# Attention with a sliding window and two MLPs: DVE's copy of the transposed probabilities and its reciprocals in front of the weight split, one more copy on ACT

## The chip, the cores and the metric

One core of one Trainium2 chip. The metric is the device time of one execution in microseconds, as the median of three runs.

## What is computed

```python
def _attn_ref(q, k, v, n_sink, window):          # q, k, v: 2 x 8 x 768 x 64; n_sink 4, window 128
    scores = np.matmul(q, k.transpose(0, 1, 3, 2)) / np.sqrt(D)
    keep = is_sink | in_window                   # the first 4 keys, and the 128 up to the query's own
    scores = np.where(keep, scores, -1e9)
    a = np.exp(scores - np.max(scores, axis=-1, keepdims=True))
    a = a / (np.sum(a, axis=-1, keepdims=True) + 1e-09)
    return np.matmul(a, v)

def reference(...):
    x = attn_out as 1536 tokens x 512
    h = x @ w_in;  g = elu(h);   x = g @ w_out      # 512 -> 2048 -> 512, first MLP
    h = x @ w_in2; g = max(h,0) + alpha*min(h,0)    # second MLP
    return g @ w_out2
```

The weights arrive as 64-bit floats.

## The kernel before

Queries are cut into seven blocks of 110 (the last has 108). Attention works on **units**: one or two query blocks of one pair of heads. There are 32 of them. Block 6 is a unit by itself, so units 9 and 11, for example, have one block, while units 8 and 10 have two. Each block gives two tiles, one for each head of the pair.

`fast_path` runs a loop of 34 **steps**, in an order written out by hand: each engine takes its instructions in the order in which the program issues them. In step s three units are at work:

- Unit s: PE forms the scores (L521, tiles `qk`, four PSUM buffers). DVE scales, masks and takes the maximum of each tile (L529). ACT takes the exponential and its sum (L534). Then `normalised` has DVE add 1e-9 and take the reciprocal (L544, L547, tile `st`), and POOL multiplies each tile of probabilities `s` by it (L551), two multiplications for a unit of one block and four for a unit of two.
- Unit s-1: `transposed` has PE transpose its probabilities into PSUM (L565, `t`), one tile a block. Each is copied to SBUF (`pt`, L649): the first copy of a unit on DVE, the second on ACT up to step `DS[HP]`, that is step 9, and on DVE after that.
- Unit s-2: `values` multiplies `pt` by the values (L586, `x`). ACT rounds the product to the high part (`xh`, L594), DVE takes the rest (`xl`, L596).

Beside these a step takes one piece of the first MLP from a list (`fill`): from step 5 to 12 one tile of `h` (L293, twelve matmuls; `g1`), whose ELU runs on ACT (L325, L326) and DVE (L327, tile `u`), and from step 13 on a tile of `o` (`g2`). Where there is no such piece PE is kept busy with matmuls that nothing reads. ACT rounds `u` to `gh` (L339) and POOL forms the rest `gl` (L340) at the start of the next step.

The weights of the first quarter of the first MLP are split in the same loop, eight **half slices** of 128x512, in the steps `DS = [1, 3, 5, 7, 9, 10, 11, 12]`. `decode_w` turns 64-bit floats into two 32-bit parts, high and low. It is a generator, and its pieces are issued at these places: at the end of step s-1 two operations on ACT (L267, L268), in step s four operations on DVE (L270, L273, L276, L279; tiles `wx`, `wq`), called **the split** here, and at the start of step s+1 the rounding on ACT (`wh`, L283) and the rest on DVE (`wl`, L285). On DVE the `wl` of step s stands in front of the first L529 of step s+1. The `o` of step 13 needs the half slice that is split in step 12.

On DVE a step of the list `DS` thus reads: L529 (two or four times), L596, the split, L649, L544, L547, L327, then L285 of the start of the next step. The attention and its list end near 165 us. After that the two MLPs run over token groups of 512.

Of the kernel before, what the change touches and what calls it, by code (L numbers as in the profile page):

```python
# [34 lines left out]
HP = H // 2  # L35
# [21 lines left out]
DS = [1, 3, 5, 7, 9, 10, 11, 12]  # L57
# [56 lines left out]
def attention_mlp2(  # L114
# [13 lines left out]
    nc = tc.nc  # L128
# [64 lines left out]
    def load_w(m, fc, io, raw=None):  # L193
        if raw is None:
            raw = rawp.tile([P, DM, 2], I32, tag="raw", name=f"wr{m}_{fc}_{io}")
        nc.sync.dma_start(
            out=raw, in_=weights[m][fc, io].bitcast(I32).rearrange("p (n t) -> p n t", t=2)
        )
        wraw[m, fc, io] = raw
# [18 lines left out]
    for i, most in enumerate((SINK, 0, WIN, 0)):  # L218
# [7 lines left out]
        out=flag_i, in0=int1[:, 2:3].bitcast(U32), scalar=0.5, in1=flag_m, op0=ALU.is_ge, op1=ALU.mult  # L226
# [6 lines left out]
        out=lims, in0=intf[:, :, 0], scalar=0.0, in1=intf[:, :, 1], op0=ALU.is_lt, op1=ALU.add  # L233
    )
    nc.vector.scalar_tensor_tensor(
        out=lims, in0=lims, scalar=4294967296.0, in1=intf[:, :, 0], op0=ALU.mult, op1=ALU.add
# [10 lines left out]
    def keep_busy(pool, tag, n):  # L247

        t = pool.tile([P, 512], F32, tag=tag, name=f"busy{next(ids)}")
        for _ in range(n):  # L250
            nc.tensor.matmul(t[:, :P], ident, ident, start=True, stop=True)  # L251
# [121 lines left out]
    def done(steps):  # L373
        for _ in steps:
            pass
# [116 lines left out]
    def fast_path():  # L492
# [13 lines left out]
        def scores(i):  # L506
            g, blks = units[i]
            z = sgs[g][1]
            nk, nq = KTOT[z], QTOT[z]
            sb = at.tile([P, UB, 2, WMAX], F32, tag="s", name=f"s{i}", bufs=SB)  # L510
            st = at.tile([P, 4, UB, 2], F32, tag="st", name=f"st{i}", bufs=SB)
            pts = {}
            for blk in blks:
                n, (k0, w) = NQ[blk], SPAN[blk]
                for e in range(2):


                    pts[blk, e] = pt = ps_qk.tile([P, 512], F32, tag="qk", name=f"qk{i}_{blk}_{e}")
                    a = keys[g][e * D : e * D + D]
                    q0 = (nk if e == 0 else 2 * nk - nq) + Q0[blk] - Q0[SPLIT[z][0]]  # L520
                    nc.tensor.matmul(  # L521
                        pt[:n, :w], a[:, q0 : q0 + n], a[:, k0 : k0 + w], start=True, stop=True
                    )
            soft[i] = sb, st
            for j, blk in enumerate(blks):
                n, w = NQ[blk], KW[blk]
                mask = masks[mask_of[blk]]
                for e in range(2):
                    nc.vector.tensor_tensor_reduce(  # L529
                        out=sb[:n, j, e, :w], in0=pts[blk, e][:n, :w], in1=mask[:n, :w],  # L530
                        scale=-SCALE, scalar=3.0e38, op0=ALU.add, op1=ALU.min,
                        accum_out=st[:n, 0, j, e : e + 1],
                    )
                    nc.scalar.activation(  # L534
                        sb[:n, j, e, :w], sb[:n, j, e, :w], AF.Exp, bias=st[:n, 0, j, e : e + 1],
                        scale=-1.0, accum_out=st[:n, 1, j, e : e + 1],
                    )
                yield

        def normalised(i):  # L540
            _, blks = units[i]
            n, c = NQ[blks[0]], len(blks)
            sb, st = soft[i]
            nc.vector.tensor_scalar(  # L544
                out=st[:n, 2, :c], in0=st[:n, 1, :c], scalar1=1.0e-9, scalar2=None, op0=ALU.add
            )
            nc.vector.reciprocal(st[:n, 3, :c], st[:n, 2, :c])  # L547
            for j, blk in enumerate(blks):
                w = KW[blk]
                for e in range(2):  # L550
                    nc.gpsimd.tensor_scalar(  # L551
                        out=sb[:n, j, e, :w], in0=sb[:n, j, e, :w], scalar1=st[:n, 3, j, e : e + 1],
                        scalar2=1.0, op0=ALU.mult, op1=ALU.mult,
                    )

        def transposed(i):
            _, blks = units[i]
            sb, _ = soft.pop(i)
            for j, blk in enumerate(blks):
                n, c, r = NQ[blk], NCH[blk], CR[blk]  # L560
                tp = ps.tile([P, 512], F32, tag="ps", name=f"t{i}_{blk}")
                for e in range(2):
                    for k in range(c):
                        o = (e * c + k) * n
                        nc.tensor.transpose(  # L565
                            tp[:r, o : o + n], sb[:n, j, e, k * r : k * r + r], ident[:n, :n]
                        )
                pt = at.tile([P, 4 * QB], F32, tag="pt", name=f"pt{i}_{blk}", bufs=PB)
                trans[i, blk] = pt
                yield pt[:r, : 2 * c * n], tp[:r, : 2 * c * n]  # L570

        def values(i):
            g, blks = units[i]
            b, z, hp = sgs[g]
            vr = vals[g]
            px = ps.tile([P, 512], F32, tag="ps", name=f"x{i}")
            o = 0
            for blk in blks:
                n, c, r = NQ[blk], NCH[blk], CR[blk]
                v0 = sum(NCH[SPLIT[z][0] : blk]) * 2 * D  # L580
                pt = trans.pop((i, blk))
                for e in range(2):
                    for k in range(c):
                        vs = v0 + (k * 2 + e) * D
                        p0 = (e * c + k) * n
                        nc.tensor.matmul(  # L586
                            px[e * D : e * D + D, o : o + n], vr[:r, vs : vs + D], pt[:r, p0 : p0 + n],
                            start=(k == 0), stop=(k == c - 1),
                        )
                o += n  # L590
            c0 = b * S + Q0[blks[0]]
            xh, xl = (x[:, hp, c0 : c0 + o] for x in xs)

            nc.scalar.copy(xh, px[:, :o])  # L594
            yield
            nc.vector.tensor_tensor(out=xl, in0=px[:, :o], in1=xh, op=ALU.subtract)  # L596
# [27 lines left out]
        decodes = {}  # L624
        gates = []
        for s in range(nu + 2):
            late = s - 1 in decodes
            if late:
                next(decodes[s - 1])
            for a in gates:  # L630
                done(a)
            gates = []
            if late:
                done(decodes.pop(s - 1))
            sc = scores(s) if s < nu else iter(())
            next(sc, None)
            vs = values(s - 2) if s >= 2 else iter(())
            next(vs, None)
            done(sc)
            done(vs)  # L640
            if s in decodes:
                next(decodes[s])
            take = 1 if fill and fill[0][0] <= s else 0
            after = fill.pop(0)[1]() if take else None
            if not take and s < nu:
                keep_busy(ps, "ps", BUSYN)
            if 1 <= s <= nu:
                for j, (out, in_) in enumerate(transposed(s - 1)):
                    (nc.scalar.copy if j and s <= DS[HP] else nc.vector.tensor_copy)(out, in_)  # L649
            if s < nu:  # L650
                normalised(s)
            if not take and s < nu:
                keep_busy(ps, "ps", BUSYN)
            if after:
                after = after()
                next(after)
                gates.append(after)
            if len([f for f in fill if f[0] <= s]) >= FILL_MAX:
                after = fill.pop(0)[1]()()
                next(after)  # L660
                gates.append(after)
            for blk, at_ in MS.items():
                if s == at_:
                    make_mask(blk)
            if s + 1 in DS:
                decodes[s + 1] = decode_w(at2, wa, *ws[DS.index(s + 1)])
                next(decodes[s + 1])
            if s in DS and WPRE <= DS.index(s) and DS.index(s) + 3 < len(ws):
                load_w(*ws[DS.index(s) + 3])
            if s < nu:  # L670
                g = units[s][0]
                if s == last_of[g] and HP <= g and g + LB < len(sgs):
                    load_kq(g + LB, at)
            if s >= 2:
                g = units[s - 2][0]
                if s - 2 == last_of[g] and HP <= g and g + LB < len(sgs):
                    load_v(g + LB, at)
# [153 lines left out]
```

## Time and profile before

| | us |
|---|---|
| median of 3 runs | 660.78 |
| lowest and highest | 659.86, 787.24 |
| the profiled execution | 662.34 |
| its span in the trace | 660.5 |
| PE busy in the span | 633.7 (96%) |
| DVE busy | 435.9 (66%) |
| ACT busy | 315.7 (48%) |
| POOL busy | 204.4 (31%) |

PE's share is an average over the whole span. The steps of the list `DS` lie between 10.03 and 76.49 us, a tenth of it. The granted TensorE clock over the span is 0.986 of full speed.

### The profile page before, as it was taken

What the parts mean: (1) busy time and instruction counts of PE and PEld (TensorE: products, weight loads), DVE (VectorE), ACT (ScalarE), POOL (GpSimd) and SP (SyncE); (2) the same over time, 40 slices, a digit from 0 to 9 for tenths busy, and PEclk for the clock granted to TensorE, in tenths of its full rate; (3) what the DMA queues carried; (4) which work ended last, traced back from release to release, by engine and by line L of the source; (5) the groups of instructions that cost most, each with busy time, mean ns of one, the idle gap of its engine ahead of it and who ended that gap; (6) DMA issues with size and microseconds to landing.
All of it is one profiled execution on the core that took longest, in us unless ns stands there. A gap on an engine that the chain in (4) does not pass through costs nothing.

```text
span 660.5 us, 9670 instructions
## 1 busy us (share of the span) xinstructions
PE 633.7 (96%) x3444; PEld 526.6 (80%) x3444; DVE 435.9 (66%) x927; ACT 315.7 (48%) x719; POOL 204.4 (31%) x253
## 2 busy tenths in 40 slices
PE   8986899999989899999999999999999999999996
PEld 7775688887977677888888888888888888888885
DVE  5877767655399997768465876694669673343332
ACT  4877466655588675647545733453524230110010
POOL 3354334434123321233215453332123312331130
PEclk9988799999999999999999999999999999999999
DMA  8574336500043343121112211212222000000112
GB/s 256 149 213 140 106 85 167 158 25 1 34 159 127 124 132 128 37 91 64 65 58 70 65 64 44 84 65 65 64 65 64 33 0 1 2 0 1 64 50 83
DMA packets 21659, 52.87 MB, mean 80 GB/s; under 512 B 2658, under 2 KB 9826, under 8 KB 21602
## 3 DMA queue, kind: packets, MB, share of 16 engines
q1 hardware_dynamic: 21024, 51.93, 25.8%
q8 instruction: 29, 0.48, 0.3%
q10 hardware_dynamic: 578, 0.24, 0.2%
q14 instruction: 28, 0.23, 0.1%
HBM read 49.01 MB, written 3.15 MB: 79 GB/s over the span
## 4 chain that ended last, share of the span: by engine, by line
PE 78%; DVE 13%; ACT 4%; issue 2%; POOL 1%; DMA 1%; DVEq 0%; ACTq 0%; SPq 0%; POOLq 0%
PE o L293 36%; PE h L293 34%; PE x L586 3%; DVE wx L276 3%; DVE wx L279 2%; ACT s L534 2%; PE t L565 2%; PE qk L521 2%; DVE wl L285 2%; DVE wx L273 1%; DVE wx L270 1%; DVE pt L649 1%; DVE u L327 1%; DVE acc L361 1%; PE busy L251 1%
## 5 line engine op out<-in xcount | busy, mean ns | idle before, releaser
L340 POOL TENSOR_TENSOR gl<-u,gh 128x512 fp32r<-128x512 f32 (+3 forms) x104 | 133.1, 1280 | 327.6 <-ACT gh L339 322.5
L293 PE MATMUL o<-gh,wh 128*128 128x512 f32 (+3 forms) x416 | 157.3, 380 | 5.5 <-DVE u L327 5.5
L293 PE MATMUL h<-xh,wh 128*128 128x512 f32 (+3 forms) x416 | 158.1, 380 | 1.2 <-ACT xh L594 1.2
L293 PE MATMUL o<-gl,wh 128*128 128x512 f32 (+3 forms) x416 | 156.3, 376 | 1.8 <-POOL gl L340 1.7
L293 PE MATMUL h<-xl,wh 128*128 128x512 f32 (+3 forms) x416 | 156.6, 376 | 0.1
L293 PE MATMUL h<-xh,wl 128*128 128x512 f32 (+3 forms) x416 | 156.4, 376 | 0.0
L293 PE MATMUL o<-gh,wl 128*128 128x512 f32 (+3 forms) x416 | 155.8, 375 | 0.0
L339 ACT CAST gh<-u 128x512 fp32r<-128x512 f32 (+3 forms) x104 | 60.9, 585 | 139.3 <-DVE u L335 114.2
L293 PEld LDWEIGHTS o<-gh,wh 128*128 128x128 f32 x416 | 78.4, 189 | 23.4 <-DVE u L327 8.4
L361 DVE TENSOR_TENSOR acc<-o,acc 128x512 f32<-128x512 f32 x72 | 49.2, 688 | 72.0 <-PE o L293 71.7
L293 PEld LDWEIGHTS h<-xh,wh 128*128 128x128 f32 x416 | 79.2, 190 | 16.9 <-ACT xh L594 1.3
L293 PEld LDWEIGHTS o<-gl,wh 128*128 128x128 f32 x416 | 78.8, 189 | 16.0 <-POOL gl L340 2.9
L293 PEld LDWEIGHTS h<-xl,wh 128*128 128x128 f32 x416 | 79.3, 191 | 13.6 <-DVE xl L596 0.4
L293 PEld LDWEIGHTS h<-xh,wl 128*128 128x128 f32 x416 | 79.4, 191 | 13.4
L293 PEld LDWEIGHTS o<-gh,wl 128*128 128x128 f32 x416 | 78.8, 189 | 13.5
L551 POOL TENSOR_SCALAR s<-s,st 110x250 f32<-110x250 f32 (+5 forms) x112 | 52.6, 487 | 92.3 <-DVE st L547 31.1
L283 ACT CAST wh<-wx 128x512 fp32r<-128x512 f32 x64 | 39.6, 619 | 65.6 <-DVE wx L279 31.7
L534 ACT ACTIVATE s<-s,st 110x250 f32<-110x250 f32 (+5 forms) x112 | 53.1, 477 | 27.1 <-DVE st L529 27.0
L331 DVE TENSOR_SCALAR u<-h,alpha_sb 128x512 f32<-128x512 f32 x48 | 35.9, 748 | 45.6 <-PE h L293 45.6
L279 DVE CUSTOM_DVE_ANT_0 wx<-wx,wq 128x1024 uint16<-128x1024 uint16 x64 | 59.2, 925 | 1.4
L276 DVE SCALAR_TENSOR_TENSOR wx<-wr,wx 128x512 int32<-128x512 int32 x62 | 56.6, 914 | 1.0
L285 DVE TENSOR_TENSOR wl<-wx,wh 128x512 fp32r<-128x512 f32 x64 | 46.8, 733 | 15.5 <-ACT wh L283 13.9
(56 smaller groups left out, 634.5 us busy)
## 6 DMA issues: line engine op xcount, KB each, us to landing
wr<-in_w_dram SPq DMA_DIRECT2D x62, 512.0 KB, 3.6
kq<-in_kq_dram SPq DMA_DIRECT2D x16, 237.0 KB, 4.4
vr<-in_vc_dram SPq DMA_DIRECT2D x8, 384.0 KB, 4.1
out_dram<-acc SPq DMA_DIRECT2D x12, 256.0 KB, 2.0
kq<-in_kq_dram SPq DMA_DIRECT2D x16, 180.0 KB, 3.8
vr<-in_vc_dram SPq DMA_DIRECT2D x8, 256.0 KB, 3.8
acc<-in_w_dram SPq DMA_DIRECT2D x2, 512.0 KB, 5.4
kq<-in_kq_dram SPq DMA_DIRECT2D x8, 110.0 KB, 3.4
```

Source lines behind the costliest of these rows:

```text
L276: nc.vector.scalar_tensor_tensor(out=x, in0=high, scalar=-0x40000000, in1=x, op0=ALU.bitwise_and, op1=ALU.bitwise_or)
L279: nc.vector.tensor_tensor(out=x, in0=x, in1=r, op=ALU.add)
L283: nc.scalar.copy(wh, xf)
L285: nc.vector.tensor_tensor(out=wl, in0=xf, in1=wh, op=ALU.subtract)
L293: nc.tensor.matmul(out, a, c, start=(i == 0), stop=(i == n - 1))
L331: nc.vector.tensor_scalar(out=u, in0=hp, scalar1=0.0, scalar2=alpha_sb[:, fc : fc + 1], op0=ALU.min, op1=ALU.mult,)
L339: nc.scalar.copy(gh, u)
L340: nc.gpsimd.tensor_tensor(out=gl, in0=u, in1=gh, op=ALU.subtract)
L361: nc.vector.tensor_tensor(out=a, in0=po, in1=a, op=ALU.add)
L534: nc.scalar.activation(sb[:n, j, e, :w], sb[:n, j, e, :w], AF.Exp, bias=st[:n, 0, j, e : e + 1], scale=-1.0, accum_out=st[:n, 1, j, e : e ...
L551: nc.gpsimd.tensor_scalar(out=sb[:n, j, e, :w], in0=sb[:n, j, e, :w], scalar1=st[:n, 3, j, e : e + 1], scalar2=1.0, op0=ALU.mult, op1=ALU. ...
L586: nc.tensor.matmul(px[e * D : e * D + D, o : o + n], vr[:r, vs : vs + D], pt[:r, p0 : p0 + n], start=(k == 0), stop=(k == c - 1),)
```

## The change

The split's four operations on DVE are issued behind the copies of the transposed probabilities and behind the addition and the reciprocal, no longer ahead of them. And the second copy of a unit stays on ACT up to the last step of the list, step 12.

```diff
@@ the loop of fast_path @@
             done(sc)
             done(vs)
-            if s in decodes:
-                next(decodes[s])
             take = 1 if fill and fill[0][0] <= s else 0
             after = fill.pop(0)[1]() if take else None
             if not take and s < nu:
                 keep_busy(ps, "ps", BUSYN)
             if 1 <= s <= nu:
                 for j, (out, in_) in enumerate(transposed(s - 1)):
-                    (nc.scalar.copy if j and s <= DS[HP] else nc.vector.tensor_copy)(out, in_)
+                    (nc.scalar.copy if j and s <= DS[-1] else nc.vector.tensor_copy)(out, in_)
             if s < nu:
                 normalised(s)
+            if s in decodes:
+                next(decodes[s])
             if not take and s < nu:
                 keep_busy(ps, "ps", BUSYN)
```

On DVE, step 5: the split of the half slice `wx_2_0` and, as `pt_2` and `st_490`, the copy and the reciprocal of that step (- is before, + is now; numbers behind a name count tiles).

```order
 L596 TENSOR_TENSOR xl<-x_503,xh 128x220
+L647 COPY pt_2_534<-t_2_529 125x440
+L544 TENSOR_SCALAR st_490<-st_490 110x4
+L547 RECIPROCAL st_490<-st_490 110x4
 L270 TENSOR_SCALAR wx_2_0_482<-wx_2_0_482 128x512
 L273 TENSOR_SCALAR wx_2_0_482<-wx_2_0_482 128x512
 L276 SCALAR_TENSOR_TENSOR wx_2_0_482<-wr_2_0_184,wx_2_0_482 128x512
 L279 ISA wx_2_0_482<-wx_2_0_482,wq_2_0_483 128x1024
-L649 COPY pt_2_538<-t_2_533 125x440
-L544 TENSOR_SCALAR st_490<-st_490 110x4
-L547 RECIPROCAL st_490<-st_490 110x4
```

Three operations moved from behind the split to in front of it. The other seven steps of the list change in the same way.

On DVE, step 11, the only one in which a copy changes its engine (units 9 and 11, copied in steps 10 and 12, have one block each).

```order
 L596 TENSOR_TENSOR xl<-x_974,xh 128x108
+L647 COPY pt_4_999<-t_4_994 128x440
+L544 TENSOR_SCALAR st_965<-st_965 108x2
+L547 RECIPROCAL st_965<-st_965 108x2
 L270 TENSOR_SCALAR wx_2_1_954<-wx_2_1_954 128x512
 L273 TENSOR_SCALAR wx_2_1_954<-wx_2_1_954 128x512
 L276 SCALAR_TENSOR_TENSOR wx_2_1_954<-wr_2_1_721,wx_2_1_954 128x512
 L279 ISA wx_2_1_954<-wx_2_1_954,wq_2_1_955 128x1024
-L649 COPY pt_4_1003<-t_4_998 128x440
-L649 COPY pt_5_1010<-t_5_1005 125x440
-L544 TENSOR_SCALAR st_965<-st_965 108x2
-L547 RECIPROCAL st_965<-st_965 108x2
```

Beside the three that moved, the copy `pt_5` is gone from DVE.

On ACT, step 11, where that copy stands now.

```order
 L534 ACTIVATE s_964,st_965<-s_964,st_965 108x242 x2
 L594 CAST xh<-x_974 128x108
-L325 ACTIVATE u_220_2_1016<-h_220_2_985 128x220
+L647 COPY pt_5_1006<-t_5_1001 125x440
+L325 ACTIVATE u_220_2_1016<-h_220_2_981 128x220
 L326 ACTIVATE u_220_2_1016<-u_220_2_1016 128x220
```

It stands in front of the two operations of the ELU, L325 and L326. PE's and POOL's instructions keep their order.

## Rows read from the trace of the kernel before

**Rows 1.** The chain of work that ended last, in order of time, for the stretch up to 200 us: start us, us, engine, tile, line. The last five pieces are of steps 12, 13 and 14.
```profile
74.18 0.69 DVE wx L279
74.87 0.53 DVE pt L649
75.45 0.99 PE x L586 x8
76.44 2.83 PE o L293 x12
...
83.46 1.53 PE o L293 x12
```

**Rows 2.** Waits in the stretch 0 to 200 us, longest in total first: who waited, what ended the wait, us in total, times, longest us.
```profile
PE x L586 <- DVE pt L649: 10.8, 9, 3.5
```

**Rows 3.** Busy time by stretch: from and to, length, busy us and instructions of PE, PEld, DVE, ACT and POOL, granted TensorE clock, DMA share, GB/s.
```profile
76.00:80.00 4.00, 4.00 (x23) 3.74 (x20) 1.50 (x6) 1.92 (x7) 2.89 (x5) 0.50 0.67 207
...
100.00:128.00 28.00, 28.00 (x268) 23.57 (x266) 20.81 (x88) 18.68 (x68) 13.49 (x29) 1.00 0.60 159
```

**Rows 4.** The timeline on DVE (start us, us, engine, line, operation, tiles, count, and in brackets the idle time before it and what ended it): the first L529 reduction of steps 1 to 9, of step 12 and of step 13.
```profile
10.03 0.26 DVE L529 CUSTOM_DVE_ANT_0 s<-qk,mask 110x110 f32<-110x110 f32 x1
...
15.23 0.26 DVE L529 CUSTOM_DVE_ANT_0 s<-qk,mask 110x110 f32<-110x110 f32 x1
...
18.42 0.26 DVE L529 CUSTOM_DVE_ANT_0 s<-qk,mask 110x110 f32<-110x110 f32 x1
...
24.04 0.41 DVE L529 CUSTOM_DVE_ANT_0 s<-qk,mask 110x250 f32<-110x250 f32 x1
...
27.64 0.42 DVE L529 CUSTOM_DVE_ANT_0 s<-qk,mask 110x250 f32<-110x250 f32 x1 [0.45 <-PE qk L521]
...
33.80 0.41 DVE L529 CUSTOM_DVE_ANT_0 s<-qk,mask 110x250 f32<-110x250 f32 x1
...
37.96 0.41 DVE L529 CUSTOM_DVE_ANT_0 s<-qk,mask 110x250 f32<-110x250 f32 x1
...
44.53 0.42 DVE L529 CUSTOM_DVE_ANT_0 s<-qk,mask 110x256 f32<-110x256 f32 x1
...
50.14 0.40 DVE L529 CUSTOM_DVE_ANT_0 s<-qk,mask 108x242 f32<-108x242 f32 x1
...
70.43 0.41 DVE L529 CUSTOM_DVE_ANT_0 s<-qk,mask 110x256 f32<-110x256 f32 x1
...
76.49 0.40 DVE L529 CUSTOM_DVE_ANT_0 s<-qk,mask 108x242 f32<-108x242 f32 x1
```

**Rows 5.** The timeline on ACT: the last L534 exponential of steps 1, 3, 7 and 12.
```profile
11.55 0.47 ACT L534 ACTIVATE s<-s,st 110x220 f32<-110x220 f32 x1
...
20.43 0.48 ACT L534 ACTIVATE s<-s,st 110x220 f32<-110x220 f32 x1
...
40.65 0.49 ACT L534 ACTIVATE s<-s,st 110x244 f32<-110x244 f32 x1
...
72.61 0.49 ACT L534 ACTIVATE s<-s,st 110x250 f32<-110x250 f32 x1
```

**Rows 6.** The timeline of step 4, the hand-over of one step from ACT to DVE: its last exponential (L534) and the addition of 1e-9 on DVE (L544).
```profile
26.19 0.49 ACT L534 ACTIVATE s<-s,st 110x244 f32<-110x244 f32 x1
...
26.81 0.17 DVE L544 TENSOR_SCALAR st<-st 110x4 f32<-110x4 f32 x1 [0.29 <-ACT s L534]
```

**Rows 7.** The timeline on PE: the transposes L565 that run in steps 5, 9 and 12.
```profile
30.32 0.97 PE L565 MATMUL t<-ident,s 110*125 110x110 f32 x8
...
53.14 0.98 PE L565 MATMUL t<-ident,s 110*128 110x110 f32 x8
...
71.62 0.57 PE L565 MATMUL t<-ident,s 108*121 108x108 f32 x4
```

**Rows 8.** The timeline of the rest of step 12 on DVE and ACT: the first operation of the split (L270), the rounding on ACT (L283), the addition (L544), the ELU's combination (L327) and the low part of the weights (L285).
```profile
72.54 0.42 DVE L270 TENSOR_SCALAR wx<-wx 128x512 f32<-128x512 f32 x1
...
74.91 0.62 ACT L283 CAST wh<-wx 128x512 fp32r<-128x512 f32 x1 [1.06 <-DVE wx L279]
...
75.31 0.16 DVE L544 TENSOR_SCALAR st<-st 110x4 f32<-110x4 f32 x1
...
75.60 0.37 DVE L327 SCALAR_TENSOR_TENSOR u<-u,h 128x220 f32<-128x220 f32 x1
...
75.88 0.68 DVE L285 TENSOR_TENSOR wl<-wx,wh 128x512 fp32r<-128x512 f32 x1
```

**Rows 9.** The timeline on POOL and DVE where both work at once, and beside it POOL alone: the four L551 multiplications of step 4 (alone) and those of step 12, a gl operation of the MLP and an L279 of a weight split at 206 us, and a gl operation at 210 us.
```profile
27.38 1.82 POOL L551 TENSOR_SCALAR s<-s,st 110x250 f32<-110x250 f32 x4 [1.85 <-DVE st L547]
...
75.88 2.39 POOL L551 TENSOR_SCALAR s<-s,st 110x256 f32<-110x256 f32 x4 [4.04 <-DVE st L547]
...
205.93 1.48 POOL L340 TENSOR_TENSOR gl<-u,gh 128x512 fp32r<-128x512 f32 x1 [3.30 <-ACT gh L339]
206.29 1.67 DVE L279 CUSTOM_DVE_ANT_0 wx<-wx,wq 128x1024 uint16<-128x1024 uint16 x1
...
209.78 1.30 POOL L340 TENSOR_TENSOR gl<-u,gh 128x512 fp32r<-128x512 f32 x1 [2.38 <-ACT gh L339]
```

**Rows 10.** The timeline of steps 13 and 14: the low part of x on DVE (L596), and the value products of step 14 on PE (L586).
```profile
78.16 0.27 DVE L596 TENSOR_TENSOR xl<-x,xh 128x108 fp32r<-128x108 f32 x1 [0.94 <-ACT xh L594]
...
82.43 1.03 PE L586 MATMUL x<-pt,vr 128*64 128x110 f32 x16
```

## The prediction

> **What bounds the kernel now.** I read the chain of waits first, cut to the attention, since the change touches only steps 1 to 12, and a share over the whole span says nothing of them. In these steps the chain runs through DVE: in step 12 it goes from the split's L279 to the copy `pt`, then to PE's `x` and on to the `o` of step 13 [rows 1]. From there to the end of the attention PE is the chain, nearly without a gap: it is busy 28.00 of 28 us from 100 us on [rows 3]. So whatever steps 1 to 12 lose or gain is handed on whole to PE, at the `x` of step 14, which starts at 82.43 us [rows 10].
>
> Second, the waits: PE's `x` waited for `pt` nine times, 10.8 us in all [rows 2]. That is what the new order can give back, since in step 12 the transposes had started at 71.62, were 0.57 us long, and the copy came 3 us later, behind the split [rows 1, 7].
>
> Third, the timeline of DVE, for the length of the steps. Between the first reductions of neighbouring steps [rows 4], steps 1, 3, 5 and 7 took 5.20, 5.62, 6.16 and 6.57 us, and steps 9 to 12 together 76.49 - 50.14 = 26.35. The eight steps with a split: 49.90 us. A step without one took 3.19, 3.60, 4.16 and 5.61 (steps 2, 4, 6, 8). Each split step is one loop: reductions, exponentials on ACT, reciprocal, then `wl` in front of the next reductions. The split now fills the time in which DVE would wait for the exponentials and the transposes. That is the cover it loses.
>
> **The change part by part.** No DVE instruction but one copy is added or removed. What changes is the length of the loop, which I rebuild for each split step in three pieces.
>
> *From the first reduction to the split.* The split must now wait for the reciprocal, so for the last exponential. From that exponential's start to the addition it is 26.81 - 26.19 = 0.62 us [rows 6], from the addition to whatever follows the reciprocal 75.60 - 75.31 = 0.29 [rows 8]. With the last exponential at 11.55, 20.43, 40.65 and 72.61 [rows 5] and 0.91 behind it, the split starts 2.43, 2.92, 3.60 and 3.09 us into steps 1, 3, 7 and 12 [rows 4]. Step 10 is like 12: 3.09. In steps 5 and 9 the transposes are later than the exponentials, as the `h` ahead of them on PE waits for `xl`. They start 2.68 and 3.00 us into the step [rows 4, 7]. In step 5 I add 0.46, since the 0.45 that DVE waited there for `qk` goes [rows 4] and ACT is the one that is late. Half of the transposes is about 0.55, the copy 0.53 [rows 1], and 0.29 follows: 4.51 and 4.37. Step 11 has one block and reads like step 13: `xl` 78.16 - 76.49 = 1.67 into the step, 0.2 of it, the copy, and 0.29 [rows 1, 4, 10]: 2.70. Sum over the eight: 26.7 us.
>
> *The split itself.* From L270 to the rounding on ACT it took 74.91 - 72.54 = 2.37 us in step 12 [rows 8], with POOL idle. Eight of these are 19.0. Now POOL isn't idle: the reciprocal starts the multiplications L551, four of 1.82 / 4 = 0.455 us [rows 9], at the moment at which the split starts. The rows show what happens then. In step 12 the four took 2.39 beside `wl`, 0.57 more than alone. At 206 us an L279 met a `gl` and took 1.67 where 0.69 is usual: 0.98 lost to a POOL operation that alone is 1.30 long [rows 1, 9]. The waiting POOL operation went first, though DVE's queue was full. So the two take turns: split, L551, split, L551. Three L551 lie between the four operations in the six steps of two blocks, two in steps 9 and 11: 22 in all. No row shows an L551 holding up DVE. The bounds are nothing and its whole 0.455; by the nearest row a `gl` costs DVE about 0.3 less than its length, part of which passes while POOL waits. I take 0.27: 22 x 0.27 = 5.9 us. The split is 24.9. POOL's last L551 ends behind it, but before `wl` does, so the next step's transposes and copy don't wait for POOL.
>
> The Trainium skill has a rule on this (SBUF — State Buffer, Who interferes with whom): the port pair that VectorE and GpSimd share is held for a whole instruction and the other engine blocks fully, for VectorE operations with two inputs in SBUF or in a two-port mode. By the rule an L551 costs DVE all of its length, and the sum would be higher by 22 x 0.185 = 4.1 us. The `gl` row agrees that DVE stops, but not for the whole 1.30.
>
> *From the split to the next step.* The rounding is 0.62, `wl` holds DVE for 76.49 - 75.88 = 0.61 [rows 4, 8]. Before, the rounding ran while DVE copied; now DVE has only `u` to do meanwhile. Eight times 1.23 are 9.8 us. Behind the rounding ACT holds only `gh` and exponentials that need the next reductions anyway; behind `wl` on DVE stand those reductions, and PE's next scores wait for their buffers.
>
> Together 26.7 + 24.9 + 9.8 = 61.4 against 49.9: **+11.5 us** on DVE's loop.
>
> *The other steps.* Step 4 no longer ends in the wait for `qk`: -0.45. Step 8 took 1.45 more than step 6. Its `h` needs the `wl` of step 7, which is now later against `x`, so PE idles before it as it did; I leave it, and keep -1.45 as a bound. Steps 2 and 6 are ACT's and stay. The first reduction of step 13 is then 11.5 - 0.45 = 11.05 us late.
>
> *Given back in step 13.* Its `o` needs the `wl` that ends where that step's reductions start, but only for its last three matmuls, so the transposes are ready when `xl` is done. From the reduction it is 1.67 to `xl`, 0.2, and 0.6 for `pt`: the `x` of step 14 starts at 76.49 + 11.05 + 2.5 = 90.05, against 82.43: **+7.6 us**.
>
> *The copy on ACT* in step 11 takes 0.53 from DVE (left out above) and puts it ahead of the ELU on ACT, which has over 3 us until `u` is due behind the split. If that cover were gone it would cost 0.53 once.
>
> The profiled execution is 662.34, so 669.9 by the sum. It was 1.56 above the median of 660.78, so I name **668.4**. The bounds of L551 and of step 8 give 661.1 to 672.5 for this case.
>
> **Rivals.**
>
> *The POOL operations cost DVE nothing, or hardly.* An L551 has one input and may not hold up DVE; `wl` ran at 0.68 beside one, though it came first [rows 8, 9]. Without the 5.9, and with step 8 gaining up to 1.45, the time is 661.1 to 662.5: not slower. Against it: an operation of the split did lose time to POOL, in the row at 206 us [rows 9].
>
> *PE is the bound, not DVE's loop.* Then `x` comes 2 us earlier in each split step, and the 10.8 us of waits [rows 2] go, for 650; as `wl` still follows the split, half of it is likelier, 655. For it speaks the chain, in which PE follows DVE [rows 1]. Against it: the next reductions can't start before `wl`, and nothing in PE's earlier work lets them.
>
> *L551 blocks DVE for its whole length*: 22 x 0.455 = 10.0 in place of 5.9, so 672.5. No row decides between this and my 0.27. It is the case that the rule of the Trainium skill quoted above would make.
>
> *The clock.* From 76 to 80 us the granted clock was 0.50, after PE had waited [rows 3], the lower of its two levels. The `o` took 2.83 instead of 1.53 [rows 1]. If longer waits carry that level on through four or five more steps from 90 us on, at about 1.3 us each for the `o` alone, 668.4 becomes 674 or 675. Against it: at 83.46 the `o` took 1.53 again [rows 1].
>
> **How the numbers follow.** Forecast 0.52, POOL for nothing 0.16, PE the bound 0.12, whole blocking 0.13, clock 0.07. The range reaches from the second case, with 1.6 us below it, to just under the last: 659.5 to 674. It leaves out the PE case and most of the clock case. A change of 2%, some 13.2 us, is about what a measurement of this kernel can tell from none. Over 2% slower is above 674: the clock's 0.07 and a little of whole blocking, 0.09. Over 2% faster is below 647.6, which even the PE case reaches hardly: 0.02. That leaves 0.89.
>
> **What would show it.** Right: the split starts some 3 us into steps 10 and 12, `pt` ends before it, DVE's idle time moves to L649 and L544 (ACT's exponentials) and to L285 (ACT's rounding); PE's waits for `pt` shrink and its waits for L551 and `qk` grow; L270 to L279 and L551 get longer in the first 90 us; the first reduction of step 13 lies near 87.5 us. Wrong: that reduction at 78 or earlier, splits of 2.4 us beside L551, or steps of the list under 6.2 us.

## The result, and the profile after

| | before | after |
|---|---|---|
| median, us | 661.17 (4 runs) | 669.06 (4 runs, 668.31 to 670.06) |
| ratio, 95% interval | | 1.0128 [1.0113, 1.0142] |
| profiled execution, us | 662.34 | 670.06 |
| its span, us | 660.5 | 668.3 |

One of the four runs before took 787.24 us, which the ratio leaves out; the median of the other three is 660.78.

The change makes the kernel slower, by 1.3% or some 8.4 us. The loss is made in steps 1 to 12, as the first L529 reductions of steps 1 to 9, 12 and 13 on DVE show (start us, us, engine, line, operation). They answer to [rows 4].

```profile
9.34 0.26 DVE L529 CUSTOM_DVE_ANT_0 s<-qk,mask 110x110 f32<-110x110 f32 x1
...
15.56 0.27 DVE L529 CUSTOM_DVE_ANT_0 s<-qk,mask 110x110 f32<-110x110 f32 x1
...
19.12 0.27 DVE L529 CUSTOM_DVE_ANT_0 s<-qk,mask 110x110 f32<-110x110 f32 x1 [0.29 <-PE x L586]
...
25.60 0.41 DVE L529 CUSTOM_DVE_ANT_0 s<-qk,mask 110x250 f32<-110x250 f32 x1
...
28.68 0.42 DVE L529 CUSTOM_DVE_ANT_0 s<-qk,mask 110x250 f32<-110x250 f32 x1
...
37.41 0.41 DVE L529 CUSTOM_DVE_ANT_0 s<-qk,mask 110x250 f32<-110x250 f32 x1
...
41.55 0.41 DVE L529 CUSTOM_DVE_ANT_0 s<-qk,mask 110x250 f32<-110x250 f32 x1
...
49.21 0.42 DVE L529 CUSTOM_DVE_ANT_0 s<-qk,mask 110x256 f32<-110x256 f32 x1
...
55.03 0.40 DVE L529 CUSTOM_DVE_ANT_0 s<-qk,mask 108x242 f32<-108x242 f32 x1
...
77.11 0.42 DVE L529 CUSTOM_DVE_ANT_0 s<-qk,mask 110x256 f32<-110x256 f32 x1
...
84.29 0.40 DVE L529 CUSTOM_DVE_ANT_0 s<-qk,mask 108x242 f32<-108x242 f32 x1
```

From step 1 to step 13 it is 84.29 - 9.34 = 74.95 us, where it was 76.49 - 10.03 = 66.46 [rows 4]: 8.49 more. (Step 1 itself begins 0.69 earlier in this trace. The executions below begin it anywhere from 9.21 to 10.06; h and j, whose programs are those of the kernel before up to that point, at 9.47 and 9.70. So that is not the change.) Subtracting neighbours gives the steps:

| step | 1 | 3 | 5 | 7 | 9 to 12 | the eight | 2, 4, 6, 8 |
|---|---|---|---|---|---|---|---|
| before | 5.20 | 5.62 | 6.16 | 6.57 | 26.35 | 49.90 | 16.56 |
| after | 6.22 | 6.48 | 8.73 | 7.66 | 29.26 | 58.35 | 16.60 |

All of it is in the steps with a split. Over the whole stretch from step 1 to step 13 DVE was busy for 56.66 us and idle for 18.29, where it was 53.41 and 13.05: 3.25 us of the loss are longer operations, and 5.24 are waiting. Step 12 shows how, on ACT, DVE and POOL (it answers to [rows 5, 8, 9]; in brackets idle time and what ended it):

```profile
79.29 0.49 ACT L534 ACTIVATE s<-s,st 110x250 f32<-110x250 f32 x1
...
79.90 0.17 DVE L544 TENSOR_SCALAR st<-st 110x4 f32<-110x4 f32 x1
...
80.20 0.40 DVE L270 TENSOR_SCALAR wx<-wx 128x512 f32<-128x512 f32 x1
80.48 2.86 POOL L551 TENSOR_SCALAR s<-s,st 110x256 f32<-110x256 f32 x4 [2.78 <-DVE st L547]
...
80.63 0.61 DVE L273 TENSOR_SCALAR wx<-wx 128x512 int32<-128x512 int32 x1
81.28 0.84 DVE L276 SCALAR_TENSOR_TENSOR wx<-wr,wx 128x512 int32<-128x512 int32 x1
...
82.15 0.85 DVE L279 CUSTOM_DVE_ANT_0 wx<-wx,wq 128x1024 uint16<-128x1024 uint16 x1
...
83.03 0.62 ACT L283 CAST wh<-wx 128x512 fp32r<-128x512 f32 x1 [2.51 <-DVE wx L279]
...
83.68 0.69 DVE L285 TENSOR_TENSOR wl<-wx,wh 128x512 fp32r<-128x512 f32 x1 [0.39 <-ACT wh L283]
```

The last exponential starts at 79.29, the addition follows at 79.90, and only then does the split start: 80.20 - 77.11 = 3.09 us into the step, where it was 2.11. POOL's multiplications run beside it: the four take 2.86 us, and 1.82 alone [rows 9]. L273, L276 and L279 take 0.61, 0.84 and 0.85 us for the 0.43, 0.69 and 0.69 that they take without POOL (the row of L279 in [rows 1]; the other two further down). ACT waits 2.51 us for the split and rounds, and DVE waits 0.39 for the rounding before `wl`. Before, ACT waited 1.06 us there and DVE not at all: `wl` followed on `u` at once [rows 8].

In step 5 the transposes come on top (PE and DVE; it answers to [rows 7]):

```profile
31.88 0.97 PE L565 MATMUL t<-ident,s 110*125 110x110 f32 x8
...
32.51 0.62 DVE L647 COPY pt<-t 125x440 f32<-125x440 f32 x1 [1.00 <-PE t L565]
...
33.33 0.40 DVE L270 TENSOR_SCALAR wx<-wx 128x512 f32<-128x512 f32 x1
```

DVE stands idle for 1.00 us until half of the transposes is there. Before, the split ran in that time.

The waits of the first 200 us (who, for what: us in total, times, longest) answer to [rows 2]:

```profile
ACT wh L283 <- DVE wx L279: 15.0, 8, 2.5
...
PE x L586 <- DVE pt L647: 4.4, 6, 1.3
...
DVE wl L285 <- ACT wh L283: 4.1, 8, 1.1
```

PE's wait for `pt` fell from 10.8 to 4.4 us, as the new order is built to do. It did not shorten the steps: PE got its `x` sooner and then waited for other things behind DVE's loop, 3.1 us for the reductions before new scores and 2.8 for a rounding, two waits that the kernel before doesn't show. ACT waited 15.0 us for the split, DVE 4.1 for the rounding.

In steps 13 and 14 PE looks like this, with DVE's two copies of `pt` (it answers to [rows 10]):

```profile
83.70 0.55 PE L293 MATMUL o<-gh,wh 128*128 128x220 f32 x1 [0.64 <-ACT wh L283]
...
84.78 1.77 PE L565 MATMUL t<-ident,s 110*128 110x110 f32 x8
...
86.16 1.13 DVE L647 COPY pt<-t 128x440 f32<-128x440 f32 x2
86.48 2.03 PE L521 MATMUL qk<-kq 64*110 64x256 f32 x8
...
88.44 1.69 PE L586 MATMUL x<-pt,vr 128*64 128x110 f32 x16
```

The `o` gets the weights of step 12 at 83.70. The `x` of step 14 starts 88.44 - 9.34 = 79.10 us behind step 1, where it was 82.43 - 10.03 = 72.40 [rows 4, 10]: 6.70 more. Before, the same transposes and the scores behind them were:

```profile
79.06 1.78 PE L565 MATMUL t<-ident,s 110*128 110x110 f32 x8
...
80.77 1.73 PE L521 MATMUL qk<-kq 64*110 64x256 f32 x8
```

So these eight transposes ran at the lower of the clock's two levels in both kernels; those of step 9 took 0.98 [rows 7]. New in the changed kernel is that the lower level lasts longer: the scores of step 14 take 2.03 us instead of 1.73, and the `x` behind them 1.69 instead of 1.03 [rows 10]. From 44 to 100 us (columns as in [rows 3]; the clock is the third from the end) the stretch was, before:

```profile
44.00:100.00 56.00, 48.08 (x406) 40.57 (x403) 39.62 (x146) 34.87 (x119) 22.02 (x42) 0.85 0.44 128
```

and after:

```profile
44.00:100.00 56.00, 47.01 (x346) 37.99 (x342) 39.87 (x128) 33.26 (x108) 21.29 (x34) 0.79 0.39 117
```

The granted clock fell from 0.85 to 0.79. By the `x` of step 15 (86.11 before, 92.77 after) the loss is 83.43 - 76.08 = 7.35 us. It stays that up to the first L267 after the attention (175.09 and 181.76: 7.36). The last 1.1 us of this execution's difference come from behind that, where the clock was 0.95 from 165 to 200 us (before: 1.00). Three other executions of the same kernel were faster by 0.4 to 1.8 us, at a mean clock of 0.983 to 0.985 against its 0.978.

### The profile page after: what moved, and what is told of

Read it like the earlier page. It is cut to its first block, busy times and chain, and to the rows that moved or that the text cites. A ratio compares the mean times of both kernels' runs of the same rounds, so it can differ in the third digit from the quotient of the medians.

```text
span 668.3 us, 9668 instructions
## 1 busy us (share of the span) xinstructions
PE 640.5 (96%) x3444; PEld 531.5 (80%) x3444; DVE 438.7 (66%) x926; ACT 315.9 (47%) x720; POOL 208.4 (31%) x253
## 3 DMA queue, kind: packets, MB, share of 16 engines
q1 hardware_dynamic: 21024, 51.93, 24.9%
## 4 chain that ended last, share of the span: by engine, by line
PE 79%; DVE 12%; ACT 5%; issue 2%; DMA 1%; POOL 1%; DVEq 0%; ACTq 0%; SPq 0%
PE o L293 36%; PE h L293 34%; PE x L586 3%; ACT s L534 3%; PE t L565 3%; DVE wx L276 2%; PE qk L521 2%; DVE wx L279 2%; DVE wl L285 1%; DVE wx L273 1%; DVE wx L270 1%; DVE pt L647 1%; DVE acc L361 1%; DVE u L327 1%; ACT wh L283 1%
## 5 line engine op out<-in xcount | busy, mean ns | idle before, releaser
L551 POOL TENSOR_SCALAR s<-s,st 110x250 f32<-110x250 f32 (+5 forms) x112 | 55.5, 513 | 87.8 <-DVE st L547 42.2
L283 ACT CAST wh<-wx 128x512 fp32r<-128x512 f32 x64 | 39.7, 620 | 76.6 <-DVE wx L279 42.7
L534 ACT ACTIVATE s<-s,st 110x250 f32<-110x250 f32 (+5 forms) x112 | 53.1, 476 | 26.5 <-DVE st L529 26.4
L279 DVE CUSTOM_DVE_ANT_0 wx<-wx,wq 128x1024 uint16<-128x1024 uint16 x64 | 60.0, 938 | 1.3
L285 DVE TENSOR_TENSOR wl<-wx,wh 128x512 fp32r<-128x512 f32 x64 | 46.7, 731 | 18.6 <-ACT wh L283 17.1
L276 DVE SCALAR_TENSOR_TENSOR wx<-wr,wx 128x512 int32<-128x512 int32 x62 | 57.4, 927 | 1.0
```

The source lines that it names most:

```text
L276: nc.vector.scalar_tensor_tensor(out=x, in0=high, scalar=-0x40000000, in1=x, op0=ALU.bitwise_and, op1=ALU.bitwise_or)
L279: nc.vector.tensor_tensor(out=x, in0=x, in1=r, op=ALU.add)
L283: nc.scalar.copy(wh, xf)
L285: nc.vector.tensor_tensor(out=wl, in0=xf, in1=wh, op=ALU.subtract)
L534: nc.scalar.activation(sb[:n, j, e, :w], sb[:n, j, e, :w], AF.Exp, bias=st[:n, 0, j, e : e + 1], scale=-1.0, accum_out=st[:n, 1, j, e : e ...
L551: nc.gpsimd.tensor_scalar(out=sb[:n, j, e, :w], in0=sb[:n, j, e, :w], scalar1=st[:n, 3, j, e : e + 1], scalar2=1.0, op0=ALU.mult, op1=ALU. ...
```

## Experiments

Each kernel was timed in five rounds against the kernel before; the ratio is to that kernel. "1 to 13" is the time from the first reduction of step 1 to that of step 13 in its profile.

| kernel | median, us | ratio, 95% interval | 1 to 13, us |
|---|---|---|---|
| a_order: the order alone | 669.35 | 1.0131 [1.0117, 1.0146] | 84.98 - 9.60 = 75.38 |
| b_copy: the copy alone | 661.37 | 1.0004 [0.9989, 1.0018] | 77.63 - 10.03 = 67.60 |
| c_mid: copies, split, addition | 663.47 | 1.0045 [1.0033, 1.0058] | 79.39 - 9.55 = 69.84 |
| d_narrow_after: POOL's work cut, order after | 664.18 | 1.0062 [1.0044, 1.0080] | 80.11 - 9.43 = 70.68 |
| e_narrow_before: POOL's work cut, order before | 660.79 | 0.9989 [0.9975, 1.0003] | 74.97 - 9.21 = 65.76 |
| f_rest_late: after, wl moved | 664.24 | 1.0051 [1.0032, 1.0071] | 78.67 - 9.42 = 69.25 |
| g_mid_last: c's order in steps 10 to 12 | 660.86 | 1.0000 [0.9988, 1.0012] | 76.56 - 10.06 = 66.50 |
| h_mid_last_rest_late: g, wl moved | 657.33 | 0.9948 [0.9931, 0.9964] | 73.62 - 9.47 = 64.15 |
| j_rest_late_before: before, wl moved | 656.95 | 0.9941 [0.9927, 0.9955] | 73.52 - 9.70 = 63.82 |

**a_order.** In the changed kernel:

```diff
-(nc.scalar.copy if j and s <= DS[-1] else nc.vector.tensor_copy)(out, in_)
+(nc.scalar.copy if j and s <= DS[HP] else nc.vector.tensor_copy)(out, in_)
```

> The new order alone; the second copy of step 11 goes back to DVE. Theory (the split lost its cover, and DVE's loop is longer): step 11 gets the 0.53 us of that copy back in its loop, so the first reduction of step 13 some 75.5 us after that of step 1 (changed kernel: 74.95; before: 66.46), and the time 0.3 to 0.6 us above the changed kernel, 8 to 9 us above the kernel before. Rival (the copy on ACT is what costs): the time falls back to within 2 us of the kernel before.

Step 11 took 7.11 us instead of 6.58, which is the 0.53 of the copy, and 1 to 13 came out at 75.38. The order is the whole loss. Nor is it the clock's: in this profile the granted clock from 44 to 100 us is that of the kernel before, 0.85, and the loss is the same.

```profile
44.00:100.00 56.00, 44.09 (x340) 35.74 (x338) 39.95 (x127) 33.07 (x108) 21.29 (x34) 0.85 0.41 116
```

**b_copy.** The same line the other way, in the kernel before.

> The kernel before with the copy alone: the second copy of step 11 on ACT, the split where it was. Theory (the two parts are independent, the copy is worth its 0.53 us on DVE in step 11): step 11 takes 6.2 instead of 6.69 us, the time is 0 to 0.6 us below the kernel before. Rival (the copy on ACT delays the ELU or the next weights and is part of the loss): step 11 or 12 longer by 0.4 us or more, the time above the kernel before.

Both expectations missed a part. The time is that of the kernel before, yet step 11 grew from 6.69 to 71.58 - 63.71 = 7.87 us. On ACT and DVE in that step:

```profile
68.08 0.53 ACT L649 COPY pt<-t 125x440 f32<-125x440 f32 x1 [2.73 <-PE t L565]
...
70.33 0.60 ACT L283 CAST wh<-wx 128x512 fp32r<-128x512 f32 x1
...
70.97 0.69 DVE L285 TENSOR_TENSOR wl<-wx,wh 128x512 fp32r<-128x512 f32 x1 [1.21 <-ACT wh L283]
```

In the old order the transposes are late in step 11, and ACT's queue holds the copy, the ELU, the next weights and the rounding in that order. The copy waits 2.73 us. The split's last operation, L279, ends at 67.53 + 0.69 = 68.22, so the rounding could have run then; it slips to 70.33, and `wl` waits 1.21 us for it. The changed kernel is spared this, as its transposes are done when ACT comes to them. So the copy wins 0.5 us in step 11 in the new order, by a_order, and loses 1.2 in the old, and the timing sees neither.

**c_mid.** In the changed kernel:

```diff
+            if s in decodes:
+                next(decodes[s])
             if s < nu:
                 normalised(s)
-            if s in decodes:
-                next(decodes[s])
```

> The split stands between the copies and the addition: copies first, then the split, then the addition and the reciprocal. Theory (what costs is that the split waits for the exponentials, that the rounding on ACT is no longer covered, and that the multiplications L551 run beside the split): all three are gone. What is left is the wait for the transposes in steps 5 and 9, about 1.0 us in step 5 and 0.2 in step 9, and it is given back by the earlier x of step 13. Steps 10 and 12 take 6.0 to 6.2 us, L270 to L279 take 2.3 to 2.4 us from the start of the first to the rounding, and the time is within 2 us of the kernel before (659 to 662). Rival (the copies in front of the split are what costs, as DVE waits for PE): nearly the whole loss stays, 667 or more.

A miss for both, nearer to the theory. The split takes 2.36 us to the rounding again in every step but the first, so POOL beside it and the wait for the exponentials are gone, and of the 1.28% 0.83 are gone with them. What stays, 0.45% or 3.0 us, is the copy in front of the split. Step 5 took 35.52 - 27.56 = 7.96 us against 6.16:

```profile
31.23 0.62 DVE L647 COPY pt<-t 125x440 f32<-125x440 f32 x1 [1.00 <-PE t L565]
...
31.77 0.42 DVE L270 TENSOR_SCALAR wx<-wx 128x512 f32<-128x512 f32 x1
...
34.13 0.62 ACT L283 CAST wh<-wx 128x512 fp32r<-128x512 f32 x1 [1.32 <-DVE wx L279]
...
35.52 0.41 DVE L529 CUSTOM_DVE_ANT_0 s<-qk,mask 110x250 f32<-110x250 f32 x1
```

It starts the split 31.77 - 27.56 = 4.21 us into the step, as the forecast's rows have it. What follows, the split, the addition, the reciprocal, `u` and `wl`, takes 35.52 - 31.77 = 3.75 us, and not the 2.95 that my 1.0 us of loss leaves for it. The other steps lose 0.3 to 0.6 each, but for step 11, which wins 0.6.

**d_narrow_after and e_narrow_before.** In the changed kernel and in the kernel before:

```diff
-out=sb[:n, j, e, :w], in0=sb[:n, j, e, :w], scalar1=st[:n, 3, j, e : e + 1],
+out=sb[:n, j, e, :8], in0=sb[:n, j, e, :8], scalar1=st[:n, 3, j, e : e + 1],
```

> The changed kernel, with the multiplications L551 on POOL over 8 columns of each tile only (the rest of the probabilities isn't normalised). To be read against the next kernel, which does the same to the kernel before. Theory: 2.8 us of the loss are POOL's L551 beside the split; the split then takes 2.4 to 2.5 us to the rounding instead of 2.55 to 2.83, and the first reduction of step 13 lies 72 to 72.7 us after that of step 1 instead of 74.95. Rival A (the multiplications beside the split are the whole loss): the difference to the next kernel vanishes. Rival B (POOL costs DVE nothing): the split stays as it is and the difference of the two stays at 8 us.

> The kernel before, with the multiplications L551 over 8 columns only (the rest of the probabilities isn't normalised). Both theories: the split has no POOL beside it, so steps 1 to 12 hardly move; the transposes come earlier where POOL was late, 0 to 3 us in all. By the theory d_narrow_after is some 5 us above this kernel, by rival A not above it, by rival B 8 us above it.

The two lie 0.73% apart, 4.8 us, as the theory had it: with POOL's multiplications cut to eight columns more than half of the loss stays, and neither rival holds. Step 12 of d (DVE, POOL, ACT):

```profile
76.50 0.40 DVE L270 TENSOR_SCALAR wx<-wx 128x512 f32<-128x512 f32 x1
...
76.79 2.17 POOL L551 TENSOR_SCALAR s<-s,st 110x8 f32<-110x8 f32 x4 [2.78 <-PE x L586]
...
76.94 0.43 DVE L273 TENSOR_SCALAR wx<-wx 128x512 int32<-128x512 int32 x1
77.40 0.69 DVE L276 SCALAR_TENSOR_TENSOR wx<-wr,wx 128x512 int32<-128x512 int32 x1
78.12 0.69 DVE L279 CUSTOM_DVE_ANT_0 wx<-wx,wq 128x1024 uint16<-128x1024 uint16 x1
...
78.85 0.62 ACT L283 CAST wh<-wx 128x512 fp32r<-128x512 f32 x1 [2.02 <-DVE wx L279]
```

The split is 78.85 - 76.50 = 2.35 us to the rounding, and no operation of it is longer than alone. 1 to 13 fell by 4.3 us, more than expected: 3.0 in the eight steps, and 1.3 in step 8, where the transposes came earlier. That was the clock: in d the matmuls of that step's `h` took 0.28 us each, in the changed kernel 0.42, at the lower level. By the times POOL's share of the loss is 8.4 - 4.8 = 3.6 us, with some 2 us of room either way by the intervals. The eight steps alone, which leave step 8 out, are the cleaner reading: they lost 58.35 - 49.90 = 8.45 us with the whole multiplications and 55.37 - 49.82 = 5.55 with the cut ones (d and e), so POOL's share there is 2.9, about what the split lost.

**f_rest_late.** In the changed kernel `wl` goes behind the reductions:

```diff
-            if late:
-                done(decodes.pop(s - 1))
             sc = scores(s) if s < nu else iter(())
...
             done(sc)
+            if late:
+                done(decodes.pop(s - 1))
```

> The changed kernel with one more move: the rest of the weights, wl (L285), stands behind the next step's reductions on DVE and no longer in front of them. Theory (DVE's loop goes through the rounding on ACT and wl, 1.26 us from the rounding's start to the next reductions, eight times): the reductions start behind u, about 0.9 us sooner, but ACT still rounds before it takes exponentials, so 0.5 to 0.7 us a step are won, and up to 1.4 in step 8 and 0.7 in step 13 are lost where h and o need wl at once. Steps 10 and 12 take 6.4 to 6.7 us instead of 7.18, the first reduction of step 13 lies 70 to 72 us after that of step 1, the time is 3 to 5 us below the changed kernel (664 to 666). Rival (the loop isn't through the rounding; the exponentials and POOL alone set it): steps of 7.1 us and a time within 1 us of the changed kernel.

The theory holds: 5.1 us below the changed kernel by the ratios. Steps 10 and 12 took 6.28 and 6.27. At the turn from step 11 to step 12, on ACT and DVE:

```profile
72.22 0.62 ACT L283 CAST wh<-wx 128x512 fp32r<-128x512 f32 x1 [1.42 <-DVE wx L279]
...
72.40 0.42 DVE L529 CUSTOM_DVE_ANT_0 s<-qk,mask 110x256 f32<-110x256 f32 x1
...
73.76 0.69 DVE L285 TENSOR_TENSOR wl<-wx,wh 128x512 fp32r<-128x512 f32 x1
```

The reductions now start 0.18 us behind the start of the rounding, where it was 84.29 - 83.03 = 1.26. The eight steps together lost 8.0 us, from 58.35 to 50.34, more than I expected. Step 8 gave 2.0 back (7.79 for 5.82), since its `h` needs the `wl` that was put off, and the copy waited long for the transposes behind it:

```profile
50.89 0.62 DVE L647 COPY pt<-t 125x440 f32<-125x440 f32 x1 [3.10 <-PE t L565]
```

**g_mid_last.** The kernel before, with c's order in steps 10 to 12 and the copy of step 11 on ACT:

```diff
-            if s in decodes:
+            if s in decodes and s < DS[5]:
                 next(decodes[s])
...
-(nc.scalar.copy if j and s <= DS[HP] else nc.vector.tensor_copy)(out, in_)
+(nc.scalar.copy if j and s <= DS[-1] else nc.vector.tensor_copy)(out, in_)
+            if s in decodes and s >= DS[5]:
+                next(decodes[s])
             if s < nu:
                 normalised(s)
```

> The kernel before in steps 1 to 9; in steps 10, 11 and 12 the copies stand before the split and the addition behind it, and the copy of step 11 is on ACT. Theory (there the transposes are ready when DVE comes to the copy, so the copy costs the loop nothing ahead of the split, and the x of step 13 comes 2 us sooner): steps 10 to 12 sum to 18.8 to 19.2 us (before: 18.85), the x of step 14 starts 4.0 us after the first reduction of step 13 (before: 5.94), and the time is 1 to 2 us below the kernel before (659 to 660). Rival (an earlier copy is hidden anyway, as PE waits for other things): the same time as before.

The steps did what was expected (6.39 + 6.11 + 6.39 = 18.89 us; the `x` of step 14 starts 80.70 - 76.56 = 4.14 behind step 13), and the time did not: it is the rival's, that of the kernel before. The start of that `x` on PE shows a part of why:

```profile
80.70 1.79 PE L586 MATMUL x<-pt,vr 128*64 128x110 f32 x16
```

It takes 1.79 us, at the lower level of the clock (0.50 from 80 to 82 us). By the next `x`, at 85.20, the gain of 1.8 us is down to 76.08 - (85.20 - 10.06) = 0.94. That is about what the interval leaves room for (0.0012 of 661 is 0.8), so whether the rest was lost stays open.

**h_mid_last_rest_late.** g with f's move, but for the half slices of steps 7 and 12:

```diff
+            soon = s - 1 in (DS[HP - 1], DS[-1])
-            if late:
+            if late and soon:
                 done(decodes.pop(s - 1))
...
             done(sc)
+            if late and not soon:
+                done(decodes.pop(s - 1))
```

> The kernel before this one, g, and the rest of the weights, wl, behind the next step's reductions, but for the half slices that h of step 8 and o of step 13 need at once. Theory: wl then fills DVE's wait for the high part of x, 0.4 to 0.9 us in most steps; the loop is shorter by 0.3 to 0.6 us in six steps, the first reduction of step 13 lies 63 to 65 us after that of step 1 (before: 66.46), and the time is 1.5 to 3 us below g. Rival (in this order DVE isn't the bound of these steps): the time of g.

3.5 us below g, a little more than expected, and faster than both kernels.

**j_rest_late_before.** The same move in the kernel before, without g.

> The kernel before with one move: wl behind the next step's reductions, but for the half slices that h of step 8 and o of step 13 need at once (the move of h, without the order of g in steps 10 to 12). Theory (h owes its 3.4 us to this move, as DVE bounds these steps and waited there for the high part of x; g alone gave nothing): the first reduction of step 13 lies 64 to 65 us after that of step 1 (before: 66.46, h: 64.15), and the time is 2 to 3.5 us below the kernel before. Rival (the two moves work only together: with the copy behind the split PE sets steps 10 to 13): the time within 1 us of the kernel before, and that of h 2 us or more below it.

As fast as h: 0.59% below the kernel before, and 1.8% below the changed one. So the gain is the move's own. By the `x` of step 15 it is 76.08 - (81.66 - 9.70) = 4.1 us. Of these 2.6 are made up to step 13; 1.5 come behind it, where the granted clock up to that `x` was 0.79, and 0.71 in the kernel before. The first reductions of steps 1 and 13 on DVE, and between them `wl` in step 12, behind the four reductions:

```profile
9.70 0.26 DVE L529 CUSTOM_DVE_ANT_0 s<-qk,mask 110x110 f32<-110x110 f32 x1
...
68.65 0.71 DVE L285 TENSOR_TENSOR wl<-wx,wh 128x512 fp32r<-128x512 f32 x1
69.28 0.37 DVE L596 TENSOR_TENSOR xl<-x,xh 128x220 fp32r<-128x220 f32 x1
69.58 0.41 DVE L270 TENSOR_SCALAR wx<-wx 128x512 f32<-128x512 f32 x1
...
73.52 0.40 DVE L529 CUSTOM_DVE_ANT_0 s<-qk,mask 108x242 f32<-108x242 f32 x1
```

`wl` is followed by `xl` and the split without a gap; in the kernel before DVE waited 0.37 us for `xh` there:

```profile
72.24 0.39 DVE L596 TENSOR_TENSOR xl<-x,xh 128x220 fp32r<-128x220 f32 x1 [0.37 <-ACT xh L594]
```

## Why the prediction was right

The forecast was 668.4 and the median is 669.06. Its mechanism holds: the split lost the cover of the exponentials and transposes, so DVE's loop got longer, and PE, which is the chain from there on, handed the loss on. Two of its sizes were off by over 2 us each, in opposite directions. That the number came within 0.7 us is therefore luck; that the kernel got slower, and where, is not.

- *First reduction to split.* Summed over the eight steps 26.7 us were forecast; 2.41, 2.65, 4.65, 3.58, 4.39, 3.09, 2.66 and 3.09 were measured: 26.5. No step is off by more than 0.3.
- *The split.* 24.9 were forecast; from L270 to the rounding it took 2.55, 2.57, 2.82, 2.82, 2.67, 2.83, 2.66 and 2.83: 21.75. Here the 5.9 us put down to POOL were mis-sized: 21.75 - 18.96 = 2.8, so 0.13 for one L551, not 0.27. Kernel d, where the split fell to 2.35, shows that POOL is what lengthens it. That the two engines take turns was half right. Their operations start in turn, DVE's at 80.20, 80.63, 81.28 and 82.15 and POOL's at 80.48, 80.94, 81.56 and 82.44 in step 12, but one doesn't wait for the other's end: alone the eight take 0.40 + 0.43 + 0.69 + 0.69 + 1.82 = 4.03 us, and here they were done in 80.48 + 2.86 - 80.20 = 3.14. I had scaled from `gl`, which is longer and of two inputs.
- *Split to the next step.* 1.23 were forecast and 1.26 measured, in every step. Kernel f, which takes `wl` out of this stretch, shows that it is on the path.
- *The other steps.* -0.45 forecast, +0.04 measured: step 4 won 0.52, step 2 lost 0.37 and step 8 lost 0.21.
- *Sum at step 13:* 11.05 late by the forecast, 8.49 measured.
- *Given back behind it:* 3.4 us were forecast for the `x` of step 14, from 2.5 us between the first reduction of step 13 and that `x`. It took 88.44 - 84.29 = 4.15, so 8.49 - 6.70 = 1.8 were given back, and 1.1 by the `x` of step 15. My path led over `xl` and `pt`, whose copies were done at 86.16 + 1.13 = 87.29, more than 1 us before the `x`. It took the transposes as ready and left out the scores of step 14, which stand in front of that `x` on PE. PE worked on both without a gap (busy for all of the 4.15 us), at the lower level of its clock, 1.77 and 2.03 us. I had that level before me for this step [rows 3] and reckoned without it.

The clock as a rival spoke of steps from 90 us on, and there it did not come: the matmuls of `o` take 0.28 us each from 90.27 on. Behind the first reduction of step 13 the lower level cost 0.30 us more than before on the scores of step 14 and 0.66 on its `x`, and not the 6 of that rival. Two of the signs failed: PE has no waits for L551, and the first reduction of step 13 came at 84.29, not near 87.5.

The other rivals: that POOL costs DVE nothing, and that it costs its whole length, are both excluded by the split's 2.82 between 2.36 and 2.36 + 3 x 0.455. By the Trainium skill's rule (SBUF — State Buffer, Who interferes with whom) the pair of ports that VectorE and GpSimd share is held for a whole instruction and the other engine blocks fully, which would be the second. The trace does not agree: L273, L276 and L279 lost 0.15 to 0.18 us each, a third or so of an L551's length, and the measurement decides. That PE is the bound is excluded by the waits: 6.4 us of PE's waits for `pt` went, and the time rose.

The loss does not need the clock: kernel a, with 0.85 from 44 to 100 us as in the kernel before, loses 1.31%. Not settled is how the level comes out in a single execution: kernel a and the changed one differ by one copy, and their profiles have 0.85 and 0.79.

## What to carry to other kernels

On an engine that takes its work in order, a block of filler that waits for nobody belongs in front of an operation that has to wait, and moving the waiting operation ahead turns the filler into part of the loop; before moving one, write down what the engine would wait for in its place. A consumer's shorter wait (PE's for `pt`) is worth nothing while the loop that feeds it is longer. The same view shows the move that does pay: `wl`, which the next reductions don't need, put behind them, won 0.59%.

## What the runs showed of the hardware

- DVE and POOL slow each other when they work side by side, and unequally. In step 12 the three operations of the split that met an L551 lost 0.15 to 0.18 us each to multiplications of 0.455, while POOL's four lost about 1.0.
- Shortening POOL's operations did not shorten their time beside DVE in proportion: in kernel d four multiplications of eight columns still took 2.17 us beside the split (2.86 with all columns) and 0.99 without it (step 4 of kernel e), though DVE lost nothing to them.
